# Eight blocks of filling matmuls that follow the token loads, and a new order table, in a one-core kernel of attention and token-mixing MLP

## The chip, the cores and the metric

The kernel runs on one core of a Trainium2 chip. The metric is device time in microseconds, the median of several executions of the whole kernel. The engines are TensorE (in the profile PE, its weight loads PEld), VectorE (DVE), ScalarE (ACT), GpSimd (POOL) and SyncE (SP), whose queue issues nearly all transfers.

## The reference, cut to what matters

S = 2048 tokens, D = 512, H = 32 heads of 16, F = 1792, inputs in bfloat16.

```python
mod = (silu(c) @ w_mod)                      # six rows of 512: sa, ca, ga, sb, cb, gb
h = layernorm(x) * (1 + ca) + sa
qkv = h @ wqkv                               # 512 -> 3*512
# each token attends to 8 tokens: itself and 2, 4, ... 14 before it (masked below 0)
x = x + ga * (attention(q, k, v) @ wo)
h = layernorm(x) * (1 + cb) + sb
u = gelu(einsum('sd,sf->df', layernorm(h), w1) + b1)     # mixes over the tokens
y = einsum('df,fs->ds', u, w2) + b2
x = x + gb * y.T
```

## The kernel before

**Tiles and chunks.** The 16 token tiles of 128 tokens are worked in five chunks (chunk 0: tiles 0 and 1, chunk 1: 2 to 5, chunk 2: 6 to 9, chunk 3: 10 to 13, chunk 4: 14 and 15). The number behind a name is the tile or the chunk.

**An order written out by hand.** The program first builds a list of some 800 named operations, with the engines that can do each and what each reads and writes. A table (`ORDER`, lines 180 to 235) then names them all in one sequence; every engine executes its own operations in just that order, and waits with semaphores for what they read. A suffix chooses the engine: `:a` ScalarE, `:d` VectorE, `:p` GpSimd, `:s` leaves a filler out, and `:q` splits a block's matmuls into four on 32 columns each. Without a suffix the first choice stands: VectorE for statistics (`ln1s`, `ln3s`) and weight scalings (`wsc`), ScalarE for normalisations (`n1_`, `n2_`, `h3_`), for evictions out of PSUM (`hT`, `ev`, `oev`, `park`) and for the residual sum `x1_`, GpSimd for the halo copies.

**The head.** SyncE loads tokens (`ld_x...`), two parts of w_mod (`ld_wmod1`, `ld_wmod0`) and the projection weights (`ld_wqkv0/1/2`); ScalarE loads c (`ld_c`). `cps` turns c into a column, `silu_exp` (ScalarE) and `silu_dve` (VectorE) make silu(c). `modcols1` and `modcols0` (TensorE) multiply it with w_mod, and VectorE takes the results as columns, `a1col` (1+ca) and `sab` (sa). For each chunk: `ln1s`, `ln1v` statistics, `rstd`, `rste`, `nb` small steps, `n1_t` normalisation, `tr` transposes on TensorE (chunks 0 and 1; `xt` by DMA for chunks 2 to 4), `hTc_k` evictions with the scale a1col. The scalings `wsc<t>_<k>` (t: 0 q, 1 k, 2 v) multiply the projection weights by a1col; chunks 2 to 4 use them, chunks 0 and 1 use the raw weights. `qvb` makes the bias from sab.

**Attention.** `qkv<c>_<t><j>` projects on TensorE, `ev` evicts. VectorE multiplies queries with shifted keys (`qk<c>_<j>`), TensorE sums groups (`red`), VectorE takes the maximum (`max`), TensorE subtracts it (`sub`), ScalarE exponentiates (`exp`), TensorE sums (`esum`), ScalarE forms the reciprocal (`rcp`, `rcq`), VectorE scales (`smB`). `a2_` and `vd` are transfers that spread weights and values, `halo_v` copies the last values of a chunk in front of the next; VectorE multiplies both (`pv`), TensorE sums (`pvacc`), `oev` evicts. `wo` projects the output; `x1_t` adds the residual: by ScalarE from PSUM, with a fifth matmul by the identity that adds x on TensorE, or (`:d`) by VectorE, without that matmul.

**MLP.** `ln2`, `n2`, `aff`, `afb`, `ln3` and `h3_t` make its input; `mlp1_<part>_<f>_<first tile>` is the first product, interleaved with attention, `park` and `padd` hold and add its parts, `gelu`; `mlp2`, `fin` and `st_out` make and store the output.

**The fillers.** A filler multiplies the identity by itself into a PSUM buffer that nobody reads. `warm0` runs 12 of them and is tied in front of `modcols1` by the key `wmA1`; of `warm1` to `warm7` the old table leaves out six and has `warm1` (2 matmuls) at its very end.

```python
for w_, n_w in enumerate(WARM):                                       # 523
    def f_warm(s_w=s_w, n_w=n_w):
        for _ in range(n_w):
            nc.tensor.matmul(ps(s_w), lhsT=ident[:], rhs=_ap(ident[:, 0:1], [[0, 4], [1, P]]), ...)
...
add("pe", 0.216 * WARM[0], f_warm0, after=[G.ops[-1]], ..., writes=["wmA1"], name="warm0")          # 538
add("pe", 0.42, lambda: f_cols(1), reads=["sc", ("wmodA", 1), "wmA1"], writes=["wmA1"], ..., name="modcols1")
```

All instructions are recorded under one line of a helper (L131), so the profile is read by tiles, not by lines: `psS` are the PSUM buffers, `big` the products, `hT` the transposed tokens, `wst`, `h` and `w_qkv` also hold weights, `xx` the tokens, `junk`, `st`, `mv`, `lv`, `rs`, `nb` the statistics.

## Time and profile before

| | us |
|---|---|
| median of 3 executions (198.60 to 198.73) | 198.67 |
| span of the profiled execution | 196.8 |
| around the span (median less span) | 1.9 |
| busy in the span: PE, DVE, ACT, POOL | 185.2, 156.6, 124.9, 19.9 |
| first matmul of a token tile | 6.47 |
| first product on VectorE | 18.07 |

Of the profiled execution the page gives the span; its time outside it is taken as the median less the span. Times in the profile count from the first instruction. A row of a timeline or a chain has the start, the duration and what ran, a row by group the count, the busy time, the mean and the idle time before. Consecutive instructions of an engine overlap a little, so that busy time divided by count is what one costs in a row of them. Matmul ends are modelled, and single matmul records can be missing.

### The profile page before, as it was taken

How to read it: one execution, taken by the hardware profiler on the slowest of the kernel's cores; microseconds unless marked ns; L12 is line 12 of the kernel's file. 1: busy time of each engine (PE TensorE's matmuls, PEld its weight loads, DVE VectorE, ACT ScalarE, POOL GpSimd, SP SyncE). 2: the span in 40 equal slices, each digit the busy share in tenths (PEclk: the TensorE clock that was granted, in tenths of full speed). 3: DMA queues.
4: the chain of work that ended last, by engine and by line, in shares of the span. 5: the costliest groups of instructions: out<-in, count | busy, mean ns of one | idle time of the engine just before them, and what ended most of it. 6: DMA issues, size and time to landing. Idle time of an engine off the chain costs nothing.

```text
span 196.8 us, 4628 instructions
## 1 busy us (share of the span) xinstructions
PE 185.2 (94%) x1850; PEld 95.5 (48%) x1867; DVE 156.6 (80%) x244; ACT 124.9 (63%) x293; POOL 19.9 (10%) x38
## 2 busy tenths in 40 slices
PE   0699999999999999899999999999999999999994
PEld 0369554654444467244544454444444444444453
DVE  2888999999999999999999999965841633453664
ACT  6877999998999999999797889812760000000000
POOL 5123006320000005030000031200000000000000
PEclk9999999999999999999999999999999999999999
DMA  5998478778899732969674768888939293001112
GB/s 169 312 366 248 115 165 256 235 216 238 165 193 317 252 131 80 312 167 249 199 200 136 159 176 180 197 250 170 336 65 309 82 257 102 30 27 53 53 53 82
DMA packets 55369, 35.95 MB, mean 183 GB/s; under 512 B 24628, under 2 KB 52788, under 8 KB 55348
## 3 DMA queue, kind: packets, MB, share of 16 engines
q1 hardware_dynamic: 53468, 34.05, 63.2%
...
q14 instruction: 7, 0.06, 0.1%
...
## 4 chain that ended last, share of the span: by engine, by line
PE 73%; DVE 13%; ACT 5%; issue 3%; DMA 2%; SPq 1%; POOL 0%; DVEq 0%; ACTq 0%
PE psS L131 71%; DVE big L131 9%; DVE h L131 2%; PE psL L131 2%; ACT junk L131 1%; SPq L131 1%; DMA vD<-v_sb 1%; ACT xx L131 1%; DMA xx<-in_A_x_dram 1%; DVE m L131 1%; ACT o_sb L131 1%; ACT lsb L131 0%; DVE mv L131 0%; POOL h L131 0%; ACT v_sb L131 0%
## 5 line engine op out<-in xcount | busy, mean ns | idle before, releaser
L131 PEld LDWEIGHTS <-wst 128*128 128x128 bf16 (+1 forms) x566 | 35.5, 100 | 31.9 <-issue 1.3
L131 PE MATMUL psS<-h,wst 128*32 128x512 bf16 (+1 forms) x400 | 50.5, 379 | 0.4 <-issue 0.3
L131 DVE TENSOR_TENSOR big<-q_sb,k_f 128x4096 bf16<-128x4096 bf16 (+1 forms) x20 | 36.4, 1857 | 0.5 <-ACT k_f L131 0.5
L131 DVE TENSOR_TENSOR big<-a2sb,vD 128x4096 bf16<-128x4096 bf16 (+1 forms) x20 | 36.6, 1858 | 0.0
L131 DVE SCALAR_TENSOR_TENSOR h<-psS,bcol,rows_bc 128x512 f32<-128x512 f32 (+2 forms) x18 | 12.4, 690 | 24.2 <-PE psS L131 24.0
L131 PE MATMUL psS<-hT,w_qkv 128*32 128x512 bf16 (+3 forms) x414 | 28.7, 337 | 0.8 <-ACT v_sb L131 0.4
L131 PEld LDWEIGHTS <-w_qkv 128*32 128x32 bf16 (+1 forms) x462 | 19.9, 108 | 16.4 <-issue 2.7
L131 PE MATMUL psS<-gT,big 128*128 128x512 bf16 x109 | 24.3, 379 | 0.2
L131 POOL TENSOR_SCALAR h<-xx,rs,nb 128x512 bf16<-128x512 bf16 x6 | 10.6, 1777 | 84.2 <-DVE nb L131 84.2
L131 PEld LDWEIGHTS <-big 128*128 128x128 bf16 x144 | 12.0, 98 | 13.7 <-issue 0.5
L131 ACT ACTIVATE junk<-xx 128x512 bf16<-128x512 bf16 x28 | 17.7, 631 | 1.3 <-DVE xx L131 0.3
L131 ACT ACTIVATE h<-xx,nb,rs 128x512 bf16<-128x512 bf16 x22 | 17.2, 818 | 0.4 <-DVE nb L131 0.4
L131 PE MATMUL psS<-woq,o_sb 128*32 128x512 bf16 (+1 forms) x123 | 15.8, 380 | 0.4 <-ACT o_sb L131 0.4
L131 ACT ACTIVATE gT<-psS,bcol 128x512 bf16<-128x512 f32 x14 | 8.8, 686 | 10.6 <-DVE psS L131 10.6
L131 DVE TENSOR_TENSOR psS<-psS,gT 128x512 f32<-128x512 f32 x14 | 9.2, 695 | 6.3 <-PE psS L131 6.3
L131 DVE TENSOR_TENSOR h<-h,xx 128x512 bf16<-128x512 f32 (+2 forms) x18 | 11.4, 633 | 0.7
L131 ACT ACTIVATE q_sb<-psS,qvb 128x512 bf16<-128x512 f32 (+1 forms) x20 | 11.6, 603 | 0.3 <-PE psS L131 0.2
L131 PEld LDWEIGHTS <-group 128*32 128x32 bf16 x288 | 7.0, 96 | 9.8 <-issue 4.0
L131 PE MATMUL psS<-hT,wst 128*128 128x256 bf16 (+2 forms) x74 | 11.3, 333 | 0.1
L131 ACT ACTIVATE v_sb<-psS,qvb 128x512 bf16<-128x512 f32 (+1 forms) x20 | 11.2, 607 | 0.0
L131 DVE TENSOR_TENSOR h<-h,rows_bc 128x1024 bf16<-128x1024 bf16 (+2 forms) x14 | 10.5, 759 | 0.0
L131 ACT ACTIVATE k_f<-psS 128x512 bf16<-128x512 f32 x16 | 9.7, 606 | 1.1 <-PE psS L131 1.1
...
## 6 DMA issues: line engine op xcount, KB each, us to landing
...
```

What stands on the lines that cost most here:

```text
L131: r = fn(*a, **k)
```

## The change

The fillers become eight blocks of 2, 1, 1, 2, 3, 3, 8 and 3 matmuls. Five of them multiply a token tile as it was loaded (`xx[:, g, :]`, tiles 1, 8, 2, 4 and 6) instead of the identity, and so start only when that load has landed; the tie by `wmA1` is gone. The table is a new one for all operations: `modcols1` stands ahead of all transposes, the seven blocks `warm1`, `warm7`, `warm0` and `warm3` to `warm6` stand ahead of it and `warm2` ahead of `modcols0`; fillers are no longer left out. GpSimd has five scalings (four before) and others of the normalisations; 37 blocks instead of 48 are split (`:q`), and seven residual sums instead of five go to VectorE. The diff, with the first 15 of the table's lines of each side:

```diff
@@ -178,60 +178,60 @@
 ORDER = """
-halo0 ident ld_c act_table cps silu_exp ld_x1 ld_x0 ln1s0 ln1v0 ln1s1:a ln1v1 rstd1_0 rste1_0 ld_x_2_8 ld_x_1_2 nb1_0
-consts ln1s9 silu_dve n1_1 n1_0:p tr0_0 ln1s8 ld_x_1_4 ln1s4:a ld_x_2_6 ln1s3:a warm0 ln1s5 ln1s7 ld_wmod1 ln1v5
-ld_wmod0 modcols1 modcols0 ln1v9 ln1v8 ln1v4 ln1s2 ln1v2 ld_wqkv0 ln1v7 ln1v3 ln1s6 ln1v6 rstd1_1 rste1_1 nb1_1 n1_4:d
-rstd1_2 rste1_2 n1_2:d n1_5:d nb1_2 ld_wqkv1 n1_3 n1_7 n1_6:d a1col hT0_2:d n1_9 tr1_2 tr1_0 hT1_1 wsc0_1:p hT0_1:d
-sab hT0_0:d ld_x_3_12 hT0_3:d hT1_3:d qvb0 qvb_cp0 qkv0_00 warm6:s wsc1_3:a hT1_2:d qkv0_02 ev0_00 ld_wqkv2 qkv0_10
-qkv0_12 ld_b2 ev0_10 ld_x_4_14 wsc1_2:p qkv0_20 wsc0_0 qvb1 ld_x_3_10 wsc0_3:p hT1_0:d ev0_02 wsc2_2:a ln1s13 ln1s12
-ev0_12 ln1v12 ln1v13 wsc1_1:a qkv0_22 qk0_1 qkv1_13 ld_wmod2 ld_wo3 qk0_0 qk0_2 n1_8 red0_0 red0_1 ln1s11:a qkv1_03:q
-qvb_cp1 qk0_3 xt6 red0_2 ld_wmod3 ev1_13 ev1_03 red0_3 mask wsc2_3:a ln1v11 ln1s10 ld_b1 ld_wo0 xt8 ev0_20 xt7 qkv1_11
-ev1_11 ln1v10 max0 qkv1_01 ev1_01 rstd1_3 ev0_22 qk1_3 xt9 sub0 exp0 qkv1_00 ev1_00 qkv1_10 ev1_10 wsc1_0:a vd0_0
-qk1_1 qkv1_02 esum0 rcp0 wsc0_2:p qk1_0 ev1_02 qkv1_12 qkv1_23 ld_wmod4 ld_wmod5 rcq0 ev1_12 qkv1_21 rste1_3 smB0
-nb1_3 a2_0_0 ln1s15:a a2_0_2 qkv2_00 qk1_2 qkv2_10 n1_13:p red1_0 ev2_00 red1_1 ev2_10 red1_2 red1_3 ln1v15 a2_0_1
-ev1_23 qkv2_13:q qk2_0 ev1_21 max1 modrow qkv1_20:q sub1:q ln1s14:a a2_0_3 pv0_0 wsc2_1:a halo_v1:a qkv1_22:q mrows
-vd0_3 vd0_1 vd0_2 ld_wo1 ev2_13 pv0_3 pvacc0_0 n1_10 exp1 ev1_20 ld_row0 qkv2_02:q pv0_1 pv0_2 warm3:s ld_wo2 esum1:q
-rcp1 ev1_22 rcq1 smB1 qkv2_03 ev2_03 pvacc0_1 pvacc0_2 xt10 wsc2_0:a pvacc0_3 ev2_02 oev0_2 qkv2_01:q vd1_3 qkv2_12
-oev0_0 ev2_01 ln1v14 qkv2_11 ev2_12 rstd1_4 qkv2_23:q n1_11 vd1_1 n1_12 a2_1_2 qkv2_22:q a2_1_3 qk2_3 woq_s rste1_4
...
+ld_c act_table ld_x1 ln1s1:a ident ld_x0 ln1s0 ln1v0 ln1v1 rstd1_0 warm1 cps rste1_0 consts ld_x_2_8 warm7 ld_x_1_2
+ld_x_1_4 ln1s8 ln1s9:a ln1s2 ln1s3 ld_x_2_6 ld_wmod1 ln1v8 ln1s4 warm0 warm3 ln1s5:a ln1v4 silu_exp ln1v3 warm4 ln1s6
+ln1v9 ln1v5 warm5 ld_wmod0 ln1v6 nb1_0 ln1s7:a ln1v2 warm6 rstd1_1 ld_wqkv0 silu_dve modcols1 ln1v7 n1_1:d rste1_1
+nb1_1 ld_wqkv1 n1_3:d n1_0:p tr0_0 rstd1_2 n1_2:d ld_x_3_12 ld_wqkv2 ld_b2 a1col rste1_2 ld_x_4_14 n1_4 warm2 modcols0
+nb1_2 n1_5:d tr1_2 hT0_0 sab n1_6:d ld_x_3_10 ld_wmod2 hT0_3 hT0_1:d hT0_2 hT1_3:d n1_8:p wsc0_3 tr1_0 n1_7:d ld_wo3
+wsc0_2:a hT1_2 wsc0_1:p ld_wo0 halo0 qvb0 qkv0_00 qvb_cp0 ev0_00 qkv0_10 hT1_0:d ev0_10 qkv0_02 qkv0_12 qkv0_22
+hT1_1:d ev0_02 wsc1_1 ln1s13 qkv0_20 xt6 n1_9:p ln1v13 ev0_12 qkv1_03 ln1s12:a qk0_1 qkv1_13 ld_wmod4 qk0_0 qvb1
+red0_0 ln1s14 wsc1_0:p qk0_2 wsc2_2:p ld_b1 red0_1 red0_2 qk0_3 wsc1_2:p red0_3 ld_wmod5 ln1s10:a xt7 ev1_03 qkv1_11:q
+xt9 ln1s11 ev1_13 mask qkv1_01 xt8 wsc1_3:a ln1s15:a ev1_11 wsc0_0:p qk1_3 ln1v15 max0 qkv1_10 qvb_cp1 ln1v12 ev1_01
+sub0 qkv1_00 qkv1_02 ev0_22 qkv1_12 exp0 esum0 ev1_00 ln1v11 ev1_10 wsc2_3:a ev1_02 qk1_1 ln1v10 rstd1_3 rcp0 rcq0
+ln1v14 ld_wo2 ld_wmod3 qkv1_20 qk1_0 rstd1_4 ev1_12 qkv1_23 ev0_20 qkv2_00 qkv2_10 red1_0 red1_1 smB0 qk1_2 red1_2
+red1_3 qkv1_21:q rste1_3 nb1_3 a2_0_3 rste1_4 vd0_0 ev2_00 a2_0_2 a2_0_1 n1_10:p halo_v1 ev2_10 nb1_4 qkv1_22:q n1_14
+wsc2_0:a qk2_0 n1_15 ev1_23 ev1_20 max1 vd0_3 ev1_21 a2_0_0 pv0_0 pv0_3 wsc2_1:a modrow sub1:q vd0_1 pv0_1 qkv2_11:q
+pvacc0_0 exp1 mrows qkv2_01:q ev1_22 esum1:q qkv2_03:q ld_wo1 vd0_2 xt10 pvacc0_1 ev2_11 ld_row0 vd1_2 rcp1 rcq1
+ev2_01 pv0_2 vd1_0 oev0_0 ev2_03 n1_11 n1_13 smB1 red2_0 qk2_1 qkv2_12:q qkv2_13:q ev2_13 woq_s qk2_3 pvacc0_2 ev2_12
...
 """
@@ -264,7 +264,8 @@
     GRP=(2, 4, 4, 2, 1),
     XDMA=(2, 3, 4),
     INJ=(),
-    WARM=(12, 2, 2, 2, 2, 2, 2, 2),
+    WARM=(2, 1, 1, 2, 3, 3, 8, 3),
+    GATE=(None, None, 1, 8, 2, 4, 6, None),
 ):
     nc = _OrderedNC(tc, 1)
     G = _Graph(dict(ps=6, big=NBIG, vd=NVD))
@@ -522,20 +523,18 @@
 
     for w_, n_w in enumerate(WARM):
         s_w = _Slot("ps")
-
-        def f_warm(s_w=s_w, n_w=n_w):
+        g_w = GATE[w_]
+
+        def f_warm(s_w=s_w, n_w=n_w, g_w=g_w):
+            rhs = _ap(ident[:, 0:1], [[0, 4], [1, P]]) if g_w is None else xx[:, g_w, :]
             for _ in range(n_w):
-                nc.tensor.matmul(ps(s_w), lhsT=ident[:], rhs=_ap(ident[:, 0:1], [[0, 4], [1, P]]), start=True, stop=True)
-        if w_ == 0:
-            f_warm0, s_w0 = f_warm, s_w
-            continue
-        G.add_any([("pe", 0.216 * n_w, f_warm), ("skip", 0.0, lambda: None)], reads=["ident"], alloc=s_w, frees=s_w,
-                  name=f"warm{w_}")
+                nc.tensor.matmul(ps(s_w), lhsT=ident[:], rhs=rhs, start=True, stop=True)
+        G.add_any([("pe", 0.216 * n_w, f_warm), ("skip", 0.0, lambda: None)],
+                  reads=["ident"] + ([] if g_w is None else [("xx", g_w)]), alloc=s_w, frees=s_w, name=f"warm{w_}")
 
     s_c, s_m = _Slot("ps"), (_Slot("ps"), _Slot("ps"))
     add("pe", 0.18, lambda: nc.tensor.matmul(ps(s_c)[:, 0:KT], lhsT=c_t[:], rhs=ident[0:KT, 0:KT], start=True,
                                              stop=True), reads=["c_t", "ident"], alloc=s_c, name="cps")
-    add("pe", 0.216 * WARM[0], f_warm0, after=[G.ops[-1]], alloc=s_w0, frees=s_w0, writes=["wmA1"], name="warm0")
     add("act", 0.2, lambda: nc.scalar.activation(ecol[:], ps(s_c)[:, 0:KT], ACT.Exp, scale=-1.0), reads=[s_c, "act_table"],
         writes=["ecol"], name="silu_exp")
 
@@ -550,10 +549,10 @@
             for kt in range(KT):
                 nc.tensor.matmul(ps(s_m[v])[:, dt_:dt_ + 1], lhsT=wmodA[:, kt, v * D + dt_ * P: v * D + (dt_ + 1) * P],
                                  rhs=sc[:, kt:kt + 1], start=(kt == 0), stop=(kt == KT - 1))
-    add("pe", 0.42, lambda: f_cols(1), reads=["sc", ("wmodA", 1), "wmA1"], writes=["wmA1"], alloc=s_m[1], name="modcols1")
+    add("pe", 0.42, lambda: f_cols(1), reads=["sc", ("wmodA", 1)], alloc=s_m[1], name="modcols1")
     add("dve", 0.15, lambda: nc.vector.tensor_scalar_add(a1col[:], ps(s_m[1])[:, 0:KT], 1.0), frees=s_m[1],
         writes=["a1col"], name="a1col")
-    add("pe", 0.42, lambda: f_cols(0), reads=["sc", ("wmodA", 0), "wmA1"], frees=s_wm, alloc=s_m[0], name="modcols0")
+    add("pe", 0.42, lambda: f_cols(0), reads=["sc", ("wmodA", 0)], frees=s_wm, alloc=s_m[0], name="modcols0")
     add("dve", 0.15, lambda: nc.vector.tensor_copy(sab[:], ps(s_m[0])[:, 0:KT]), frees=s_m[0], writes=["sab"],
         name="sab")
     scale_w(1)
```

78 lines of the change are left out of this document (39 added, 39 removed).

## The prediction

> **What bounds the kernel now.** I read the page first, then the busy time by stretch, then the chain of waits, then the timelines of the single engines.
>
> ```profile
> span 196.8 us, 4628 instructions
> PE 185.2 (94%) x1850; PEld 95.5 (48%) x1867; DVE 156.6 (80%) x244; ACT 124.9 (63%) x293; POOL 19.9 (10%) x38
> ```
>
> The span is 196.8 us and the median of the runs 198.67: some 1.9 us lie around the span, and I leave them as they are. TensorE is busy 94% of the time, so a gain must come from TensorE's idle time or from work taken off it. Busy time by stretch says where VectorE binds as well:
>
> ```profile
> 18.00:41.00 23.00, 22.84 (x285) 13.22 (x290) 22.89 (x22) 22.45 (x51) 4.91 (x1) 1.00 0.67 181
> 41.00:83.00 42.00, 40.11 (x623) 21.25 (x629) 41.93 (x35) 40.44 (x95) 3.89 (x2) 1.00 0.78 212
> 83.00:126.00 43.00, 42.65 (x497) 20.35 (x498) 42.45 (x90) 38.20 (x105) 5.11 (x6) 1.00 0.73 190
> 126.00:191.00 65.00, 64.68 (x299) 29.65 (x304) 33.64 (x51) 10.78 (x16) 0.00 (x0) 1.00 0.50 139
> ```
>
> After the stretch and its length come TensorE, weight loads, VectorE, ScalarE and GpSimd. From 18 to 83 VectorE is full (22.89 of 23, 41.93 of 42) and TensorE nearly so. From 83 on TensorE runs without a hole (42.65 of 43, 64.68 of 65), and from 126 VectorE has half its time free. So whatever brings TensorE's work at 83 forward reaches the end, but before 83 VectorE must come forward too. The chain of waits says the same:
>
> ```profile
> 6.47 10.88 PE psS L131 x108
> ...
> 17.38 0.61 ACT k_f L131
> ...
> 18.07 1.79 DVE big L131 x2
> ...
> 82.77 7.30 PE psS L131 x33
> ...
> 119.54 10.74 PE psS L131 x49
> ```
>
> It goes through TensorE from 6.47, the first key eviction at 17.38, the first VectorE product at 18.07, and is all TensorE after 82.77. The last piece gives the pace: 10.74 us for 49 matmuls of 512 columns, 0.22 us each.
>
> **The head.** TensorE's timeline:
>
> ```profile
> 6.47 1.03 PE L131 MATMUL psS<-ident,h 128*128 128x128 bf16 x8 [4.09 <-POOL h L131]
> 7.30 5.20 PE L131 MATMUL psS<-ident 128*128 128x512 bf16 x12
> 12.33 0.94 PE L131 MATMUL psS<-sc,big 128*128 128x1 bf16 x32
> 13.13 1.05 PE L131 MATMUL psS<-ident,h 128*128 128x128 bf16 x16
> 14.02 0.67 PE L131 MATMUL psS<-sab,wst 128*128 128x1 bf16 x16
> 14.55 3.66 PE L131 MATMUL psS<-hT,wst 128*128 128x256 bf16 x32
> ```
>
> These rows are tr0_0, the twelve filler matmuls of warm0, modcols1 and modcols0, both tr1, qvb0, and the first four projection blocks. The fillers cost 0.43 us each, half the pace above; at 14.55 the pace is full (3.66 for 32 of 256 columns, 0.11 each). The clock rose about 5 us after continuous work began at 7.30. The fillers hold everything back until 12.33, but the projections also need loads:
>
> ```profile
> 3.73 1.02 SPq L131 DMA_DIRECT2D big<-in_w_mod_dram  x2
> DMA to landing us min/median/max: 6.0/6.0/6.0
> 4.80 1.55 SPq L131 DMA_DIRECT2D wst<-in_A_wqkv_dram  x2
> DMA to landing us min/median/max: 7.8/8.3/8.8
> ```
>
> The first half of w_mod lands at 3.73+6.0 = 9.7. The two projection weights land at 4.80+7.8 = 12.6 and near 14.1. The table keeps SyncE's first seventeen transfers in order, so these times stay, and the head cannot gain more than 14.55-12.6-0.5 = 1.4 us (0.5 is qvb0). What fits before 12.6 goes by VectorE's queue:
>
> ```profile
> 6.06 0.38 DVE L131 TENSOR_SCALAR ecol<-ecol 128x4 f32<-128x4 f32 x1
> 6.76 2.01 DVE L131 BATCH_NORM_STATS2 st<-xx 128x6 f32<-128x512 bf16 x3
> L131 DVE BATCH_NORM_STATS2 st<-xx 128x6 f32<-128x512 bf16 x10 | 6.7, 684 | 3.5 <-DMA xx<-in_A_x_dram 3.5
> L131 DVE TENSOR_SCALAR h<-xx,mv,rs 128x512 bf16<-128x512 bf16 x4 | 1.4, 409 | 0.0
> L131 DVE TENSOR_SCALAR hT<-psS,a1col 128x512 bf16<-128x512 bf16 x3 | 1.4, 471 | 0.0
> ```
>
> silu_dve takes 6.76-6.06 = 0.7. The third of the three statistics read the token pair that lands last; it began at 6.76+2.01-0.69 = 8.08, so I take that pair to be there at 8.05. In the new queue silu_dve stands behind the statistics of that pair (8.05 to 8.7) and five small ones (0.8): it ends at 10.2. modcols1 (half of 0.94) ends at 10.7, tr0_0 at 11.2, modcols0 at 11.7. VectorE meanwhile needs three normalisations, a1col and another one, 4x0.35+0.5 with small ones, until 12.2. Then both tr1 follow (0.9, to 13.1) and qvb0 (0.5): the first projection starts at 13.6 instead of 14.55, **0.9 us earlier**. Bounds: 1.4 above, and 0.2 if the clock is still low (below).
>
> VectorE's first product needs a key and a query.
>
> ```profile
> 15.63 0.84 ACT L131 ACTIVATE q_sb<-psS,qvb 128x256 bf16<-128x256 f32 x2
> 33.57 2.28 DVE L131 TENSOR_TENSOR big<-q_sb,k_f 128x4096 bf16<-128x4096 bf16 x1
> 35.77 1.21 DVE L131 TENSOR_REDUCE m<-psL 128x128 bf16<-128x1024 f32 x1
> ```
>
> The new table projects q and k first (13.6 to 15.35), evicts in 0.84 (the query) and 0.61 (the key, chain above), and keys are there at 16.1. VectorE's own queue from 12.2 is two normalisations 0.7, four hT 1.7, two scalings 1.0, one statistic 0.67, small ones 0.3: 16.5 against 18.07, **1.5 us earlier**. Up to the first value product (pv0_0) its queue holds one statistic more (two against one) and small ones, 0.7, so 0.8 us remain. From there to the last pv2 product the queue holds the same work in another order, but the max3 reduction (1.2, as at 35.77) comes behind that product instead of ahead of it, against two small ones that come earlier: 1.1 more, so VectorE is 1.9 us ahead where TensorE takes over at 83.
>
> Four of pv0's transfers are queued differently:
>
> ```profile
> 31.27 2.70 SPq L131 DMA_DIRECT2D a2sb<-lsb  x4
> ```
>
> The last of the four a2_0 issues now comes sixth (two vd0 between), 1.3 us later after smB0 (0.65 each); I charge 0.3 us of VectorE wait, since max1 covers the rest (0 to 1.0). That leaves VectorE 1.6 us ahead at 83.
>
> **TensorE's work.** Matmuls on 32 columns (the ":q" blocks, red, pvacc) alternate with full ones:
>
> ```profile
> 39.41 0.63 PE L131 MATMUL psS<-lsb,ident 128*32 128x128 bf16 x32
> 39.98 1.05 PE L131 MATMUL psS<-hT,w_qkv 128*128 128x512 bf16 x3
> 40.96 0.40 PE L131 MATMUL psS<-big,group 128*32 128x256 bf16 x8
> L131 PE MATMUL psS<-xx,ident 128*128 128x512 bf16 x8 | 3.0, 379 | 0.0
> L131 DVE SCALAR_TENSOR_TENSOR xx<-psS,xx 128x512 bf16<-128x512 f32 x5 | 3.4, 684 | 0.1
> ```
>
> esum1 is eight steps of 0.055 from 39.41: free at 39.86, but the full block starts at 39.98. That block is four steps of 0.216 (one record is missing), free at 40.84, and the next starts at 40.96. So a change of form costs 0.12 us either way. Counted along TensorE's order, the old table changes form 26 times and the new one 16 times, all ten saved ahead of 83: **1.2 us** (0.5 if half of them hide in waits for VectorE). Seven instead of five residual sums go to VectorE (x1_9 and x1_10 added): TensorE saves two identity matmuls, **0.43 us**, and VectorE pays 2x0.68 behind 83, half of it covered by two normalisations (h3_2, h3_3) that leave its queue there, the rest by its free time from 126 on. Without that cover it would cost up to 0.7. The fillers grow from 14 to 23, but all stand in the head; the two at the old end were beside VectorE's last steps and cost nothing.
>
> **The sum**: at 83 TensorE by its own work is 0.9+1.2 = 2.1 us ahead, VectorE 1.6; the smaller counts. Behind 83 the two identity matmuls add 0.4: 2.0 in all. Span 194.8, **time 196.7 us**. All of this takes for granted that the new order adds no other wait.
>
> **GpSimd, the part that speaks against it.**
>
> ```profile
> 23.64 0.66 DVE L131 TENSOR_REDUCE m<-psL 128x64 bf16<-128x512 f32 x1
> 14.20 2.05 POOL L131 TENSOR_SCALAR w_qkv<-wst,a1col 128x512 bf16<-128x512 bf16 x3 [0.35 <-DMA wst<-in_A_wqkv_dram]
> 31.42 4.91 POOL L131 TENSOR_SCALAR h<-xx,rs,nb 128x512 bf16<-128x512 bf16 x1 [15.17 <-DVE nb L131]
> 41.01 1.21 POOL L131 COPY v_sb<-v_sb 128x64 bf16<-128x64 bf16 x1 [4.68 <-ACT v_sb L131]
> ```
>
> The old scalings ran at 0.69 each (2.05 for three) before VectorE's products began. A like operation at 31.42, under two products, took 4.91: it got on only in the reduction after them. The new queue puts n1_8, n1_9 and five scalings there in a row; the last three (wsc2_2, and behind it wsc1_2 and wsc0_0) wait for the third projection weight, around 16 (14.1 and the 1.5 that lay between the first two, and a little for the tokens between), and run into the products from 16.5 on. They need 2.1 us; VectorE's pauses between products (two statistics of 0.67, max0 0.66 with small ones 1.0, and the 0.4 before 16.5) give 2.7 us up to 26. qkv2_00 wants them at about 30. So I cost them at nothing.
>
> The Trainium skill (GPSIMD Engine Reference, Key points) says that GpSimd shares its SBUF interfaces with VectorE and contends with VectorE instructions that have two SBUF inputs. The 4.91 against 0.69 agrees; the page gives no price for it; what it would do here is the third rival.
>
> **The rivals.**
>
> *Low clock.* If waits between the gated blocks keep the clock low, the last block of eight takes 8x0.43 = 3.4 from 8.1, modcols1 starts at 11.5 instead of 10.2, VectorE's a1col slips by 0.7, and the head gains 0.2: time 197.4. For it: the blocks wait for four loads. Against it: they fill from about 2.3 on, so 5 us of work end at 7.3, before the last block. The Trainium skill (TensorE: Matmul & The Clock Gate, Part 1) has a free-running window of about 3.4 us that must be busy; by that the clock would rise between 5.7 and 9.1, an estimate, and the sum would stay as it is. The change of pace between 7.30 and 12.33 agrees with it.
>
> *VectorE sets 83.* If VectorE's lead of 0.8 at pv0_0, less 0.3, is all that passes (max3 then holds back softmax 3 and what follows), with the 0.4 from TensorE: gain 0.9, 197.8. For it: 41.93 of 42 busy. Against it: TensorE needs pv2, not max3, for the output projections at 83.
>
> *Scalings locked out (slower).* If the pauses don't do, wsc0_0 is left over at 26, and the next true pause is where VectorE runs out of input: it reaches qk2_0 (33.57 in the old queue, 15.5 behind the first product, and 0.7 more in the new one) at 16.5+16.2 = 32.7, the scaling ends at 33.3, qkv2_00 and qkv2_10 take 1.75, eviction 0.6 and hand-overs 0.3: VectorE stands from 32.7 to 36.0, 3.3 us, time 200.0. It decides at about 30, when TensorE arrives at qkv2_00. The same can happen to halo_v1, behind n1_10 on GpSimd: a copy of that size took 1.21 at 41.01, under two products. It must fit under max1 near 36, or the value transfers of chunk 1 come only when VectorE stands at pv1_0; waiting for two vd1 and four a2_1 issues and their landing is some 6 us: 202.5.
>
> *Not what it says.* Scalings on GpSimd go only from four to five; if the head is hidden and the order no better, no change: 198.7.
>
> **How the numbers follow.** This kernel's measurement can tell about 0.2% (0.4 us) from no change. Forecast 0.55, low clock 0.10, VectorE at 83 0.08, scalings locked out 0.16, halo 0.06, no change 0.05. Faster: 0.55+0.10+0.05 of the third = 0.70; same 0.05 and 0.01 of the third; slower 0.24, the rest of the third included. The likeliest is 196.7. Below: 1.4 for the head, 1.2, 0.4 and no new wait, 3.0: 195.6. Above, the range must reach to the locked scalings at 200.0; halo and what lies beyond both ends leave out about 0.15.
>
> **What would show it.** Right: first projection near 13.6 with 256-column matmuls at 0.11; first product on VectorE near 16.5; GpSimd's last early scaling done by 26; 0.12 us holes fewer by ten; the chain all TensorE from about 80.5. Wrong: qkv2_00 waiting for GpSimd, VectorE with holes between 30 and 60, fillers at 0.43 up to 11.5, or TensorE holes behind 83 (a w1 load that arrives late).

## The result and the profile after

The changed kernel takes 201.03 us (median of 4 executions, 200.39 to 201.69) against 198.63 for the kernel before beside it: ratio 1.0123, 95% interval 1.0095 to 1.0151. It is 1.2% slower, where 196.7 was forecast and the range ended at 200.0. Executions of one kernel spread here by one to two microseconds (the kernel before: 197.75 to 199.59 in another comparison), so beside each ratio I use the length of stretches inside the trace. The profiled execution after took 201.69, the slowest of the four, with a span of 199.9; a difference of spans (3.1) therefore says a little more than the medians (2.4).

The page after, span and busy time, and then the busy time by stretch (stretch, length, TensorE, weight loads, VectorE, ScalarE, GpSimd, granted clock, DMA share, GB/s):

```profile
span 199.9 us, 4311 instructions
PE 187.3 (94%) x1690; PEld 95.5 (48%) x1706; DVE 157.6 (79%) x244; ACT 124.3 (62%) x294; POOL 27.4 (14%) x44
```

```profile
18.00:41.00 23.00, 22.33 (x302) 12.57 (x305) 22.16 (x25) 21.48 (x49) 7.80 (x5) 1.00 0.69 178
41.00:83.00 42.00, 38.89 (x469) 20.65 (x463) 41.69 (x32) 37.59 (x90) 5.64 (x2) 1.00 0.73 203
83.00:126.00 43.00, 41.55 (x453) 19.79 (x455) 41.28 (x85) 37.79 (x98) 4.14 (x5) 1.00 0.60 174
126.00:191.00 65.00, 63.79 (x292) 28.89 (x297) 34.78 (x56) 13.15 (x25) 2.30 (x3) 1.00 0.56 151
```

VectorE, full before (22.89 of 23), now lacks 0.84 in the first stretch, and TensorE, which ran without a hole from 83, lacks 1.45 in the third and 1.2 in the fourth. What TensorE waited for from 14 to 197 (engine and tile, released by; total, times, longest):

```profile
PE psS L131 <- DVE big L131: 2.4, 5, 0.8
PE psL L131 <- DVE big L131: 1.2, 2, 0.9
PE psS L131 <- DMA wst<-in_B_w_dram: 0.9, 1, 0.9
PE psL L131 <- DVE m L131: 0.8, 2, 0.5
```

The chain of waits, whose last part was all TensorE from 82.77, now passes through VectorE, a transfer of softmax weights and a weight load before TensorE has it to itself at 136.37:

```profile
80.86 1.22 DVE m L131
...
89.27 0.64 SPq L131
90.62 2.38 DMA a2sb<-lsb
93.00 1.29 issue
...
97.35 6.61 DVE big L131 x3
104.78 10.82 PE psS L131 x49
...
130.32 6.00 DMA wst<-in_B_w_dram
136.37 4.49 PE psS L131 x20
```

The head did what was forecast. TensorE's timeline:

```profile
8.02 1.89 PE L131 MATMUL psS<-xx,ident 128*128 128x512 bf16 x8 [0.30 <-DMA xx<-in_A_x_dram]
10.03 0.55 PE L131 MATMUL psS<-sc,big 128*128 128x1 bf16 x16
...
13.49 1.69 PE L131 MATMUL psS<-hT,wst 128*128 128x256 bf16 x13
```

The last block of eight fillers runs at full pace (1.89), modcols1 is at 10.03, the first projection at 13.49, VectorE's first product (qk0_1) at 16.62. From there to VectorE's last partial sum (padd1_12) it takes 131.40 us, against 127.35 before: the kernel starts its products 1.45 earlier and is 2.6 late at the end. VectorE's timeline has the two largest holes, in front of pv0_2 and of pv3_2:

```profile
40.88 1.23 DVE L131 TENSOR_TENSOR big<-a2sb,vD 128x2048 bf16<-128x2048 bf16 x1 [0.84 <-PE psS L131]
...
94.38 2.29 DVE L131 TENSOR_TENSOR big<-a2sb,vD 128x4096 bf16<-128x4096 bf16 x1 [1.38 <-PE psL L131]
```

Starts of VectorE's steps in the profiled executions (us), the stretch from qk0_1 to padd1_12, and qk0_3's duration. smB1 scales softmax 1, aff2 is the first step of the MLP's input behind pv2, max4 and smB4 belong to the last softmax.

| kernel | qk0_1 | pv0_0 | smB1 | aff2 | max4 | smB4 | padd1_12 | stretch | qk0_3 |
|---|---|---|---|---|---|---|---|---|---|
| before | 18.07 | 36.91 | 41.45 | 81.08 | 94.48 | 102.89 | 145.43 | 127.35 | 1.22 |
| after | 16.62 | 36.57 | 42.03 | 81.99 | 96.66 | 105.00 | 148.02 | 131.40 | 1.63 |
| e1_head | 17.47 | 36.31 | 40.85 | 80.47 | 93.89 | 102.30 | 144.84 | 127.38 | 1.22 |
| e3_max3 | 16.49 | 36.43 | 41.65 | 81.62 | 95.42 | 103.76 | 146.40 | 129.91 | 1.63 |
| e4_red2 | 16.87 | 36.81 | 41.36 | 81.71 | 96.05 | 104.38 | 146.35 | 129.48 | 1.63 |
| e5_ld | 16.04 | 35.99 | 42.31 | 82.33 | 96.65 | 104.99 | 146.94 | 130.90 | 1.64 |
| e6_three | 16.09 | 36.05 | 40.60 | 80.95 | 94.75 | 103.09 | 145.04 | 128.95 | 1.64 |
| e8_wsc | 16.54 | 37.29 | 41.85 | 82.23 | 96.04 | 104.38 | 146.33 | 129.79 | 1.22 |
| e10_pool40 | 16.03 | 35.98 | 41.43 | 81.40 | 95.94 | 104.28 | 146.37 | 130.34 | 1.63 |
| e13_head3 | 16.62 | 36.25 | 40.78 | 80.42 | 93.81 | 102.23 | 144.75 | 128.13 | 1.23 |
| e16_pvacc | 15.76 | 35.73 | 40.27 | 80.61 | 95.16 | 103.50 | 145.57 | 129.81 | 1.63 |

By segments, after less before: +1.11 to pv0_0, +0.92 to smB1 (the hole of 0.84), +0.33 to aff2, +1.27 to max4 (the hole of 1.38), -0.07 to smB4, +0.48 to padd1_12 (the load): 4.04 in all. Another 0.5 lies behind the last store.

The stretch of the new order is not a fixed length. e10_pool40 has the same table as the kernel after (only four fills move to another engine), and its stretch is 1.06 shorter: 0.12 in the segment to max4 and 0.93 in the last one, while the other four segments agree to 0.01. The old order repeats its stretch to 0.03 in four executions (before, e1, e9, e14). So for a repair of the new order the segment that it touches says more than the whole stretch.

### The profile page after: what moved, and what is told of

It reads as the page before. It is cut to its first block, busy times and chain, and to the rows that moved or that the text cites. A ratio compares the mean times of both kernels' runs of the same rounds, so it can differ in the third digit from the quotient of the medians.

```text
span 199.9 us, 4311 instructions
## 1 busy us (share of the span) xinstructions
PE 187.3 (94%) x1690; PEld 95.5 (48%) x1706; DVE 157.6 (79%) x244; ACT 124.3 (62%) x294; POOL 27.4 (14%) x44
## 4 chain that ended last, share of the span: by engine, by line
PE 56%; DVE 17%; DMA 11%; issue 6%; SPq 4%; ACT 3%; DVEq 0%
PE psS L131 54%; DVE big L131 9%; DMA wst<-in_B_w_dram 6%; SPq L131 4%; DMA wst<-in_A_wqkv_dram 4%; DVE h L131 4%; PE psL L131 2%; DVE m L131 2%; DVE st L131 1%; DMA a2sb<-lsb 1%; ACT junk L131 1%; ACT v_sb L131 1%; ACT xx L131 1%; DVE mv L131 1%; DVE lsb L131 1%
## 5 line engine op out<-in xcount | busy, mean ns | idle before, releaser
L131 DVE TENSOR_TENSOR big<-q_sb,k_f 128x4096 bf16<-128x4096 bf16 (+1 forms) x20 | 37.1, 1872 | 0.0
L131 PE MATMUL psS<-hT,w_qkv 128*32 128x512 bf16 (+3 forms) x296 | 29.2, 345 | 0.2
L131 POOL TENSOR_SCALAR h<-xx,rs,nb 128x512 bf16<-128x512 bf16 x8 | 12.4, 1556 | 91.4 <-DVE nb L131 36.8
L131 ACT ACTIVATE junk<-xx 128x512 bf16<-128x512 bf16 x30 | 18.8, 627 | 0.9 <-DMA xx<-in_A_x_dram 0.2
L131 PE MATMUL psS<-woq,o_sb 128*128 128x512 bf16 (+1 forms) x75 | 15.6, 379 | 0.1
L131 ACT ACTIVATE h<-xx,nb,rs 128x512 bf16<-128x512 bf16 x18 | 14.3, 810 | 2.1 <-DVE nb L131 2.1
L131 PE MATMUL psS<-big,group 128*32 128x512 bf16 (+1 forms) x160 | 10.0, 339 | 2.5 <-DVE big L131 2.4
## 6 DMA issues: line engine op xcount, KB each, us to landing
vD<-v_sb SPq DMA_DIRECT2D x8, 268.5 KB, 2.4
```

The costliest lines, as they stand in the source:

```text
L131: r = fn(*a, **k)
```

## The experiments

In the diffs a line stands for a piece of the table; unless said otherwise the base is the kernel after.

**The head alone.** e1_head: the new table up to qkv0_00, then the old one.

```diff
-halo0 ident ld_c act_table ... qvb0 qvb_cp0 | qkv0_00 ... (old)
+ld_c act_table ld_x1 ln1s1:a ... halo0 qvb0 | qkv0_00 ... (old)
```

> The order table of the kernel before from the first projection (qkv0_00) on, with the head of the changed kernel in front of it: the gated fillers, modcols1 ahead of the transposes, and the engines that the changed table gives to the head's steps; the four GpSimd scalings of the change are not in it. Theory A (the changed table places TensorE's steps of the later stages so that they reach VectorE's or a load's result too early; the head itself is a gain): 0.6 to 1.4 us below the kernel before, 197.2 to 198.0. Theory B (a lead at the head is used up at the next wait for VectorE, whatever stands behind it): 198.4 to 198.9, no change. Theory C (the head itself costs, because VectorE gets more of the early statistics): above 199.

198.53 against 198.51, ratio 1.0007 (0.9989 to 1.0026). In the trace the first product is 0.60 earlier than before, and every later step 0.58 to 0.61 earlier, to the end. So the loss is not in the head, and a lead passes whole where the order behind it is unchanged; but in the median no gain shows.

**The late load.** e2_load moves the matmuls that wait for it ahead of others; e5_ld moves two loads of w2 behind it.

```diff
 # e2_load
-ld_w2_0 mlp1_2_2_11 ... ld_w1_2_640 mlp1_1_11_10 padd1_11
+ld_w2_0 mlp1_1_11_10 padd1_11 mlp1_2_2_11 ... ld_w1_2_640
 # e5_ld
-padd1_10 ld_w2_0 mlp1_2_2_11 ld_w2_3 ... gelu2 ld_w1_2_640
+padd1_10 mlp1_2_2_11 ... gelu2 ld_w1_2_640 ld_w2_0 ld_w2_3
```

> The changed kernel with mlp1_1_11_10 and padd1_11 moved ahead of mlp1_2_2_11, so that TensorE has 1.3 us of matmuls more in front of the step that waits for the load ld_w1_2_0. Theory A: the hole at 135.1 (1.06 between starts, 0.22 of it a missing record) goes, and nothing behind it on TensorE waits: 0.6 to 0.9 us below the changed kernel, 200.1 to 200.4 beside 201.0. Theory B (the hole comes back behind it, at the next load or at the tail): within 0.2 of the changed kernel.

> The changed kernel with the loads ld_w2_0 and ld_w2_3 behind ld_w1_2_640 in SyncE's queue, as the kernel before has them: the load ld_w1_2_0 that TensorE awaits at 135 then moves alone. Theory A (it lands late because the two loads behind it share the DMA engines): 4.4 to 4.7 us from issue to landing instead of 6.0, the hole of 0.84 gone, 0.5 to 0.9 us below the changed kernel's 201.0. Theory B (whatever TensorE waits for there is replaced, as a PSUM wait replaced it when mlp1_1_11_10 was moved): within 0.3.

e2_load: 201.0, ratio 1.0123 (1.0095 to 1.0151), no gain in the median; the wait for the load is replaced by one of 0.4 for a gelu, a hole of 0.60 behind the matmul at 137.3. The stretch of its trace is 0.58 shorter all the same. e5_ld: 200.46, ratio 1.0112 (1.0095 to 1.0129); the interval overlaps that of the kernel after, so the median does not show the repair. In the trace the wait is gone. TensorE's timeline from 126 to 138, first of the kernel after, then of e5_ld:

```profile
125.81 9.66 PE L131 MATMUL psS<-h,wst 128*128 128x512 bf16 x43
136.37 1.90 PE L131 MATMUL psS<-h,wst 128*128 128x512 bf16 x8 [0.90 <-DMA wst<-in_B_w_dram]
```

```profile
125.80 12.47 PE L131 MATMUL psS<-h,wst 128*128 128x512 bf16 x56
```

The 800 KB load, 6.0 from issue to landing after, takes 4.7 in e5_ld and 4.6 before (the views of DMA issues from 122 to 138, in that order):

```profile
wst<-in_B_w_dram SPq DMA_DIRECT2D x1, 800.0 KB, 6.0
```

```profile
wst<-in_B_w_dram SPq DMA_DIRECT2D x1, 800.0 KB, 4.7
```

```profile
wst<-in_B_w_dram SPq DMA_DIRECT2D x1, 800.0 KB, 4.6
```

The last segment is 1.07 shorter than in the kernel after, the whole stretch only 0.50, because in this execution the hole in front of pv0_2 is 1.70. That the two loads of w2 made the load late is not shown. In eight of the profiled executions they are issued 0.42 and 0.99 behind it, and it takes 4.95 to 6.02; in three of these (e4, e10 and e16, 4.95 to 5.07) TensorE does not wait for it. One of the three, e10, has the very order of the kernel after (TensorE's timeline from 126 to 138):

```profile
125.74 12.60 PE L131 MATMUL psS<-h,wst 128*128 128x512 bf16 x56
```

Without the two beside it the load takes 4.67 to 4.94 in e5, e6, e8 and e12, but 5.49 in e7, where TensorE waits 0.4 for it. So the wait of 0.90 comes in some executions of the new order and not in others; what decides it stays open.

**Softmax 3.** e3_max3 puts max3 ahead of the last pv2 product again, and the steps to smB3 with it.

```diff
-pv2_3 pvacc2_3 pv2_1 ... pvacc2_1 max3 aff2 ... rcp3 ... rcq3 ... vd3_3 smB3
+pv2_3 pvacc2_3 max3 pv2_1 ... pvacc2_1 aff2 ... smB3 (behind the first ln3s) ... vd3_3
```

> The changed kernel with the softmax of chunk 3 in the kernel before's place: max3 ahead of the product pv2_1, sub3 ahead of pvacc2_1, exp3, esum3, rcp3 and rcq3 as early as that allows, and smB3 ahead of the statistics ln3s4, ln3s3, ln3s5 (it then starts near 84.5 instead of 87.83, and the transfers a2_3 with it). Theory A: the 1.38 us for which VectorE stands in front of pv3_2 go, and with them TensorE's holes at 95.65, 98.9 and 103.5 (0.87, 0.49, 0.28); pvacc2_1 comes up to 1.2 later, and sub3's hole of 0.69 goes: 0.8 to 1.6 us below the changed kernel. Theory B (VectorE stays as far behind at max4 and the pv3 products for its own work): within 0.3 of the changed kernel.

199.91, ratio 1.0075 (1.0050 to 1.0100); the stretch falls by 1.49, of which 0.87 in the segment to max4. The rest lies where the edit changes nothing: 0.24 to smB1 (a smaller hole in front of pv0_2) and 0.37 in the last segment. smB3 starts at 84.75 instead of 87.83, and the hole in front of pv3_2 shrinks from 1.38 to 0.11. VectorE's timeline of e3_max3 (its max3, smB3 and pv3_2):

```profile
78.29 1.22 DVE L131 TENSOR_REDUCE m<-psL 128x128 bf16<-128x1024 f32 x1
...
84.75 0.93 DVE L131 TENSOR_TENSOR lsb<-lsb,rb 128x1024 bf16<-128x1024 bf16 x1
...
93.14 2.29 DVE L131 TENSOR_TENSOR big<-a2sb,vD 128x4096 bf16<-128x4096 bf16 x1
```

The segment to max4 takes 13.80 to 13.81 in all five executions with this edit (e3, e6, e7, e8, e12), and 14.25 to 14.67 in the eight that have the new order there. In these eight pv3_2 starts 0.18 after the last of the transfers a2_3 has landed, although the row of the kernel after names TensorE. The edit moves max3, smB3 and the five steps between them; which of them counts was not separated.

**The hole in front of pv0_2.** e4_red2 moves two steps of TensorE, e16_pvacc and e17_red2only one each; e18_xt10 moves a transposing transfer instead.

```diff
 # e4_red2 (both), e16_pvacc (first), e17_red2only (second)
-pv0_1 qkv2_11:q pvacc0_0 exp1
+pv0_1 pvacc0_0 qkv2_11:q exp1
-smB1 red2_0 qk2_1 qkv2_12:q qkv2_13:q ev2_13
+smB1 qk2_1 qkv2_12:q qkv2_13:q red2_0 ev2_13
 # e18_xt10
-ld_wo1 vd0_2 xt10 pvacc0_1 ev2_11 ld_row0
+ld_wo1 vd0_2 pvacc0_1 ev2_11 ld_row0 xt10
```

> The changed kernel with two steps of TensorE moved between 38 and 47 us: pvacc0_0 ahead of qkv2_11 (it frees the buffer for which VectorE stands 0.84 us in front of pv0_2), and red2_0 behind qkv2_13 instead of ahead of qkv2_12 (TensorE stands 1.09 us there for the product qk2_1). Theory A: VectorE is 0.8 earlier from pv0_2 on and TensorE's hole goes: 0.7 to 1.1 us below the changed kernel. Theory B (TensorE's time is lost again at the next products that it waits for, at 71 to 81 us): within 0.3 of the changed kernel, with larger holes there.

> The changed kernel with pvacc0_0 ahead of qkv2_11, and nothing else moved (red2_0 stays). Theory A (VectorE sets the end of the stages up to 83, so its wait of 0.84 in front of pv0_2 is what counted in e4_red2): pv0_2 directly behind pv0_1, each later step of VectorE 0.6 to 0.8 earlier against the first product than in the changed kernel, and 0.5 to 1.0 us below the changed kernel. Theory B (TensorE's hole in front of red2_0 counts): no gain, within 0.3.

> The changed kernel with red2_0 behind qkv2_13, and nothing else moved (pvacc0_0 stays). Theory A: TensorE's hole of 1.09 us goes, VectorE's wait in front of pv0_2 stays, and with it the time, within 0.3 of the changed kernel. Theory B (TensorE's hole counts): 0.6 to 1.1 us below the changed kernel.

> The changed kernel with the transposing transfer xt10 one place later in SyncE's queue, behind ld_row0 instead of in front of it (it waits there until 39.5, so that vd0_2 has 3 us without it). Theory A (VectorE's wait in front of pv0_2 is for the transfer vd0_2, which lands late because xt10's transfers run beside it): vd0_2 lands 2.3 to 3.2 us after its issue instead of 4.3, pv0_2 starts directly behind pv0_1, and the stretch from the first product to the last partial sum, 131.40 us in the changed kernel, is 0.5 to 0.9 shorter; the time 0.4 to 0.9 below the changed kernel's. Theory B (the wait is for TensorE, for the buffer): the wait stays at 0.5 to 0.9 us, and so does the time.

| | ratio (95%) | vd0_2, issue to landing | hole before pv0_2 | stretch |
|---|---|---|---|---|
| after | 1.0123 (1.0095 to 1.0151) | 4.26 | 0.84 | 131.40 |
| e4_red2 | 1.0084 (1.0054 to 1.0113) | 3.01 | none | 129.48 |
| e16_pvacc | 1.0101 (1.0065 to 1.0137) | 3.14 | none | 129.81 |
| e17_red2only | 1.0150 (1.0118 to 1.0182) | 3.96 | 0.55 | 130.72 |
| e18_xt10 | 1.0132 (1.0100 to 1.0165) | 4.59 | 1.19 | 131.42 |

The place of pvacc0_0 decides about the hole. In all six executions with it ahead (e4, e6, e7, e8, e12, e16) vd0_2 takes 3.01 to 3.14 and there is none; in all seven with it behind (after, e2, e3, e5, e10, e17, e18) vd0_2 takes 3.96 to 5.12 and the hole is 0.55 to 1.70. The stretches hold more than that: in e4 and e16 the segment to smB1 is 0.91 shorter, the next one 0.37 to 0.38 longer (in e16 VectorE now waits 0.27 in front of aff0), and the last one 1.05 and 0.95 shorter, which is the w1 load, landed in time without an edit to it.

Two things in the expectations were wrong. TensorE's hole of 0.91 behind smB1 is in front of red2_1, which waits for the product qk2_1, not of red2_0, so moving red2_0 leaves a hole of 0.63 there (e17). And pv0_2 does not wait for a buffer that pvacc0_0 frees: where the transfer vd0_2 is late enough, the profile names it (VectorE's timeline of e18_xt10):

```profile
41.55 1.23 DVE L131 TENSOR_TENSOR big<-a2sb,vD 128x2048 bf16<-128x2048 bf16 x1 [1.19 <-DMA vD<-v_sb]
```

In after, e17 and e18 pv0_2 starts 0.12 after vd0_2 lands (40.76, 40.28, 41.43), and 0.12 to 0.13 after it in the other four executions with the hole, so the name "PE psS" in the row of after is that of another wait of the same instruction, which ended a little earlier. What holds vd0_2 back is not xt10. The views of DMA queues and issues around it, first e18_xt10 (36.8 to 42), then e16_pvacc (35.6 to 40.8):

```profile
GB/s 314 446 347 446 330 149 110 181 252 221 441 352 371 397 347 231 132 66 17 0 0 0 0 17 17 0 17 0 17 17 33 80 134 95 165 197 185 248 244 250
...
q8 instruction: 1, 0.02, 1.9%
...
vD<-v_sb SPq DMA_DIRECT2D x1, 268.5 KB, 4.6
```

```profile
q8 instruction: 1, 0.02, 1.4%
...
vD<-v_sb SPq DMA_DIRECT2D x1, 268.5 KB, 3.1
```

In e18 the rate falls to 0 to 17 GB/s from 39.1 to 40.7: 15 of the 16 parts of vd0_2 have landed by 39.71, the last comes at 41.43. In the packets' times one instruction packet of 16 KB lies beside it, from 38.21 to 39.83 (in after from 37.77 to 39.07); in e16 and e4 it starts at 38.60 and 39.58, 0.2 before vd0_2 lands. In all thirteen executions the packet starts 1.3 to 2.5 after the issue of vd0_2 where that is late, and 2.8 to 3.0 after it where it is not. That the packet holds the transfer up would fit this. That it is the cause, and why a step of TensorE moves it, was not tried and stays open.

**Three repairs together.** e6_three has the edits of e3, e4 and e5; e7_stats moves two statistics of it to ScalarE; e8_wsc takes from e6 all scalings off GpSimd that ran under VectorE's products.

```diff
 # e7_stats, on e6_three (the small steps ln1v14 to nb1_4 and n1_14, n1_15 go later)
-red0_0 ln1s14 wsc1_0:p ... xt9 ln1s11 ev1_13
+red0_0 wsc1_0:p ... xt9 ln1s11:a ev1_13 ... ev1_21 ln1s14:a
 # e8_wsc, on e6_three
-wsc1_0:p ... wsc2_2:p ... wsc1_2:p ... wsc0_0:p
+wsc1_0:a ... wsc2_2:a ... wsc1_2:a ... wsc0_0
```

> The changed kernel with three repairs together: pvacc0_0 and red2_0 moved (38 to 47 us), the softmax of chunk 3 in the kernel before's place, and the two loads of w2 behind ld_w1_2_640. Theory A (each hole counts by itself, they add): 201.0 less 1.1, 1.1 and 0.5 to 0.8, so 198.0 to 198.4. Theory B (they overlap: the lead of the first is lost at the second's place): 199.0 to 199.6. Theory C (the head's lead comes out as well, now that it isn't lost behind): 197.0 to 197.8.

> The kernel with the three repairs, and the statistics ln1s11 and ln1s14 on ScalarE as in the kernel before (two statistics of 0.68 us less on VectorE between 18.9 and 22.8), with what hangs on ln1s14 (ln1v14, rstd1_4, rste1_4, nb1_4, n1_14, n1_15) moved behind smB1. Theory A (VectorE sets the end of the stages up to 83, so its work there counts): 0.6 to 1.3 us below the kernel with three repairs. Theory B (TensorE is busy without a break from 26 to 41 and sets that stretch, so VectorE's lead is turned into a wait): within 0.3. Theory C (ScalarE's evictions come later): slower by 0.3 to 1.

> The kernel with the three repairs, and no weight scaling on GpSimd during the products: wsc1_0, wsc1_2 and wsc2_2 on ScalarE, wsc0_0 on VectorE. Theory A (the scalings on GpSimd cost what the slowed product qk0_3 shows, 1.63 us instead of 1.21): qk0_3 back at 1.21, but 0.42 more for wsc0_0 on VectorE, so within 0.3 of the kernel with three repairs. Theory B (the scalings on GpSimd slow more than that): over 0.4 us faster. Theory C (three scalings of about 0.7 us on ScalarE push its evictions back, and the projections wait for PSUM buffers): 0.5 to 1.5 us slower, that is, the change's use of GpSimd was a gain.

e6_three: 199.08, ratio 1.0046 (1.0017 to 1.0075), stretch 128.95. Of the stretch's 4.05 too much 2.45 are gone, and about two thirds of the loss in the median. Its segments less those of before are +1.12 to pv0_0, +0.01, +0.72, +0.40, -0.07, and -0.59 to padd1_12. Against the kernel after its gains are 0.91 to smB1, with 0.38 lost in the next segment, 0.87 to max4 and 1.07 in the last: those of the single repairs, each in its own segment.

e7_stats: 204.28, ratio 1.0258 (1.0220 to 1.0296), much worse. What VectorE waited for from 16 to 84:

```profile
DVE nb L131 <- ACT rs L131: 2.6, 1, 2.6
DVE big L131 <- ACT k_f L131: 1.6, 1, 1.6
DVE mv L131 <- ACT xx L131: 0.7, 1, 0.7
```

The two statistics cost VectorE 0.7 each, but on ScalarE they hold back a key's eviction and come late themselves. The run shows that these two places on ScalarE are bad, not that no place is good.

e8_wsc: 199.93, ratio 1.0077 (1.0060 to 1.0094). qk0_3 is back at 1.22, yet the stretch is 0.84 longer than e6's, for VectorE now waits 0.9 for a key and TensorE 1.5 for a maximum. Of this 0.80 lies in the segment to pv0_0, which takes 19.94 to 19.97 in the eleven executions with the new order there. By the trace GpSimd's scalings are a gain on balance, although they slow a product; the intervals of the medians overlap.

**The head with the early projections.** e11_head2 has the new order up to qk0_1 and then the old one; e13_head3 lets ln1v12, which waits for a statistic on ScalarE, follow ln1v11; e15_head4 moves ln1s11 and ln1v11 as well.

```diff
 # e13_head3, on e11_head2
-ln1v12 ... qk0_0 ... ln1v11 ln1s10
+qk0_0 ... ln1v11 ln1v12 ln1s10
 # e15_head4, on e13_head3
-red0_1 ln1s11:a qvb_cp1 qk0_3 ... ev1_03 ... ln1v11 ln1v12 ... max0
+red0_1 qvb_cp1 qk0_3 ... ev1_03 ln1s11:a ... ln1v12 ... max0 ln1v11
```

> The changed kernel's order up to VectorE's first product (qk0_1), and from there on the kernel before's order. In the earlier kernel with the changed head (up to qkv0_00) the first product began at 17.47, since ScalarE had n1_9, hT1_1 and wsc1_3 ahead of the evictions and VectorE two statistics ahead of the product, and every later step was 0.6 earlier than in the kernel before, to the end. Theory A (VectorE's lead at the first product is carried whole to the end where the order behind it is the kernel before's): first product at 16.4 to 16.9, 0.8 to 1.5 us below the kernel before. Theory B (the lead varies with the landing of the first loads and is gone in the median, as in that kernel): within 0.4 of the kernel before.

> The same as e11_head2 (the changed kernel's order up to the first product qk0_1, then the kernel before's), with ln1v12 moved from in front of qk0_0 to behind ln1v11, so that VectorE doesn't stand 1.2 us for ScalarE's statistic ln1s12 there. Theory A (with the kernel before's order behind it, the lead that VectorE has at the products of chunk 0 is carried step by step to the end): qk0_0 near 17.9 instead of 19.26, each later step 0.7 to 1.3 us earlier than in the kernel before, and the time 0.6 to 1.2 us below it. Theory B (the next wait, the evictions of qkv1 for qk1_3, takes it back): steps from qk1_3 on within 0.3 of the kernel before, and no change in the time.

> The kernel e13_head3 with ScalarE's statistic ln1s11 moved behind the evictions ev1_13 and ev1_03, and VectorE's ln1v11 behind max0 (in e13_head3 VectorE stood 0.19 us for it, and the evictions came 1.46 us later for it). Theory A (VectorE's lead is carried whole): steps from qk1_3 on 0.2 to 0.5 earlier against the first product than in e13_head3, and 0.4 to 0.9 us below the kernel before. Theory B (the median of the kernel before already holds most of that lead, since its clock rises earlier in most executions than in the profiled one): 0.1 to 0.4 below the kernel before.

e11_head2: 199.02, ratio 1.0028 (1.0004 to 1.0053). The lead of 1.62 at the first product is lost at once. VectorE's waits from 16 to 84:

```profile
DVE mv L131 <- ACT junk L131: 1.2, 1, 1.2
```

e13_head3: 197.99 against 198.30, ratio 0.9988 (0.9959 to 1.0018): the lowest median, but it cannot be told from no change. In its trace 0.67 of the lead of 1.45 comes through to the end. e15_head4: 198.77, ratio 1.0022 (1.0003 to 1.0042); the statistic moved once more is waited for again (0.6). A head that is 1.5 early needs ScalarE's statistics 1.5 earlier too.

**The close of the program.** Behind the last store GpSimd clears semaphores and drains. The drain ends 0.54 after the clear in the kernel after, 0.07 before. The kernel after has 44 GpSimd instructions on the page, the one before 38. e9_before44 and e14_before44b add six fills to the kernel before; e10_pool40 and e12_three40 move four fills of after and of e6_three to VectorE.

```diff
 # e9_before44 (in the setup) and e14_before44b (at the end of consts), on the kernel before
+for _ in range(6): nc.gpsimd.memset(epscol[:], EPS)
+for _ in range(6): nc.gpsimd.memset(onecol[64:96], 1.0)
 # e10_pool40; e12_three40 on e6_three
-nc.gpsimd.memset(mask[:, w, 0:DIL * w], MASKVAL)
+(nc.gpsimd if w < 4 else nc.vector).memset(mask[:, w, 0:DIL * w], MASKVAL)
```

> The kernel before with six more memsets of a 128x1 constant on GpSimd in the first 3 us (it then has 44 GpSimd instructions in the profile, as the changed kernel has, instead of 38), which nothing waits for. Theory A (the close of the program takes 0.49 us longer where GpSimd has 44 instructions: from the end of the semaphore clear to the end of GpSimd's next DRAIN it was 0.54 us in the changed kernel and its variants with 44, and 0.07 in the kernel before with 38 and the variant with 40): 0.54 us in that place, and 0.3 to 0.6 us above the kernel before. Theory B (it hangs on what GpSimd does in the middle of the program, the scalings, not on their number): 0.07 us there, no change in the time.

> The changed kernel with four of the mask's memsets on VectorE instead of GpSimd (40 GpSimd instructions instead of 44); the scalings stay on GpSimd. Theory A: 0.07 us at the close instead of 0.54, and 0.3 to 0.6 us below the changed kernel, about 200.5 where that takes 201.0. Theory B: 0.54 us at the close, no change.

> The kernel with the three repairs (order at 38 to 47 us, chunk 3's softmax, two loads of w2) and 40 GpSimd instructions. Theory A (the waits found and the close of the program make up the whole loss): 0.4 below the kernel with the three repairs, so within 0.3 of the kernel before. Theory B (the close doesn't count): 0.4 to 0.9 above the kernel before, like the kernel with the three repairs.

> The kernel before with six more memsets on GpSimd, at the end of its constants (3.5 us), where it idles up to 5.6 us and they wait for nothing: 44 GpSimd instructions instead of 38. Theory A (the close of the program is longer by 0.47 us from some number of GpSimd instructions between 40 and 44 on): 0.54 us from the end of the semaphore clear to the end of the next DRAIN instead of 0.07, every step before that at its old place, and the time 0.3 to 0.6 us above the kernel before. Theory B (the close was longer for another reason): 0.07 us there and no change.

e9_before44: 200.56, ratio 1.0094 (1.0061 to 1.0126), but it measures something else as well: its fills wait for ScalarE's use of epscol and hold up n1_0, the first product comes at 19.82, and the delay of 1.75 is carried to the end (1.74 to 1.78). e14_before44b, whose fills wait for nothing: 198.31 against 198.30, ratio 1.0007 (0.9985 to 1.0030). e10_pool40: 201.11, ratio 1.0115 (1.0075 to 1.0156). e12_three40: 199.76, ratio 1.0057 (1.0028 to 1.0085). The traces agree without exception: with 44 GpSimd instructions the drain ends about 0.5 after the clear (0.56 in e14), with 40 or fewer 0.07. The medians do not show it: they cannot tell half a microsecond from none.

## Why the prediction was wrong

**The head: right in the trace, with some luck, and less was to be had.** modcols1 10.03 (10.2 forecast), first projection 13.49 (13.6), first product 16.62 (16.5), and the low clock did not come (1.89 for the last eight fillers). But both ends of this lead are single draws. I took the first projection weight as landing at 12.6. In the thirteen executions with this head it lands between 11.73 and 13.31 (12.89 in the one above), and the first product follows it by 3.7 to 3.8 each time, between 15.49 and 17.04. The 18.07 from which I took the lead is one draw too. In e14_before44b, whose head is that of before but for six fills on GpSimd, TensorE came to full pace earlier; the granted clock reads 1.00 in all these rows, so only the pace shows it (TensorE's timeline):

```profile
7.39 4.32 PE L131 MATMUL psS<-ident 128*128 128x512 bf16 x12
```

Twelve fillers take 4.32 instead of 5.20, and the first product comes at 17.30. The medians of e1 and e13 bound what the new heads bring: between a loss of 0.5 and a gain of 0.8. The forecast booked 0.9 and 1.5 from a single profile.

**VectorE's lead at pv0_0: 0.34 instead of 0.8.** I counted one more statistic and small ones (0.7); the stretch grew by 1.11. The rest is qk0_3, 1.63 instead of 1.22 (VectorE's timeline of after has qk0_2 and qk0_3 together; two of these products take 2.35 undisturbed in e13_head3):

```profile
19.48 2.76 DVE L131 TENSOR_TENSOR big<-q_sb,k_f 128x2048 bf16<-128x2048 bf16 x2
```

GpSimd's scalings run beside it, and I had costed them at nothing. I had asked only whether VectorE would lock GpSimd out, not whether GpSimd would slow VectorE. They slow it in one place only. Scalings also run beside qk0_1, qk0_0 and qk0_2, which take 1.21 to 1.22 as they do alone; qk0_3 is the product during which one scaling ends and the next begins (21.15). So it is in all eleven executions with this order; in e7 that moment falls into qk0_2, and there qk0_2 takes 1.63 and qk0_3 1.21. In e8, without the scalings, qk0_3 takes 1.22. Why it happens only there was not tried. The Trainium skill (GPSIMD Engine Reference, Specifications) has the two engines share their SBUF interfaces, with contention where a VectorE instruction has two SBUF inputs, as these products have. The trace agrees for one of the four products, 1.63 against 1.22.

**"No other wait": the step that failed most.** The forecast held only if the new order added no other wait, and it added three on the path: 0.84 in front of pv0_2, 1.38 in front of pv3_2, 0.9 for a w1 load. The first two are in every execution with the new order at their place (0.55 to 1.70 in seven, 0.97 to 1.38 in eight); the third is not, e10 has none. I had allowed 0.3 for a2_0's fourth issue, which made no wait; the transfer that did, vd0_2, I had not timed. The late load stands among my signs of being wrong ("a w1 load that arrives late") without a price or a chance.

**max3: the wrong sign.** I booked max3's place behind the last pv2 product as 1.1 of VectorE's lead. It moves work past the point where I measured, and takes none off the queue. At the start of the last pv2 product, where I had VectorE 1.6 ahead, it was 0.22 ahead (78.66 against 78.88); behind max3, at aff2, it was 0.91 late. What the move also shifts is the start of softmax 3, smB3 (VectorE's timelines, first of before, then of after):

```profile
83.69 0.69 DVE L131 TENSOR_TENSOR lsb<-lsb,rb 128x1024 bf16<-128x1024 bf16 x1
```

```profile
87.83 0.69 DVE L131 TENSOR_TENSOR lsb<-lsb,rb 128x1024 bf16<-128x1024 bf16 x1
```

With it go the transfers a2_3, of which the last lands at 94.2, 0.18 before pv3_2 starts. The rival "VectorE sets 83" says that max3 then holds back softmax 3, but I priced it as a smaller gain, not as a wait. e3_max3, which undoes this with the steps behind it, gets 0.87 back in the segment to max4.

**TensorE's saved work: right, and mostly worth nothing.** The forms change 16 times instead of 26 in the trace, as counted, but ahead of 83 VectorE sets the pace and the 1.2 never shows. Behind 83 it counts: in e6, without the late load, the last segment is 0.59 shorter than before, where I had 0.43 for the two identity matmuls. x1_9 costs VectorE 0.68 ahead of that, covered by two normalisations that left, as forecast.

**The rivals.** The scalings were not locked out. GpSimd's groups by shape from 16 to 24 in the kernel after:

```profile
L131 POOL TENSOR_SCALAR w_qkv<-wst,a1col 128x512 bf16<-128x512 bf16 x2 | 3.4, 1702 | 0.0
L131 POOL TENSOR_SCALAR w_qkv<-h,a1col 128x512 bf16<-128x512 bf16 x1 | 2.7, 2690 | 1.4 <-DMA h<-in_A_wqkv_dram 1.4
```

They take 1.70 and 2.69 instead of 0.69, but the last ends at 22.80, and from 14 on no wait of TensorE is put down to GpSimd. halo_v1 took 0.23 at 36.11. So the slower case came about, by none of the mechanisms that I had given a price.

**What accounts for it.** Shown by undoing, each in the segment that it touches and against the kernel after: pvacc0_0 0.91, less the 0.38 that is lost behind it, and softmax 3 0.87 (0.45 against the least of the eight executions without this edit). The late load is worth 1.07, but not shown by undoing, for 0.93 of it goes in e10 without an edit. That makes 2.47, and e6, with all three edits, gets 2.45 back, so none takes from another. The whole stretches are 1.92, 1.49 and 0.50 shorter, 3.91 in all, because they hold differences between executions too: in e4 the load came in time (1.05), in e5 the hole in front of pv0_2 was larger (0.86). In the medians no single repair stands clear of the kernel after (its interval begins at 1.0095; those of e3 and e4 end at 1.0100 and 1.0113); e6 does, with 1.0075. Of the 1.6 that e6 keeps, 1.1 lie ahead of pv0_0 (two statistics for one, and qk0_3), 1.1 between smB1 and max4, and 0.66 come back behind. Of that middle part the waits that VectorE has left are 0.3 and 0.2 in the profile; the rest was not settled. No kernel here beats both tables by a margin that the measurement can tell.
